# Eight heads' key sums inverted together on 128x128, and GpSimd dividing in the output's stage

## The chip, the cores and the metric

The kernel runs on one core of a Trainium2 chip. The metric is the device time of one execution in microseconds; of a kernel the median of several runs is given. The profile is that of one execution, taken by the hardware profiler. The engines are called PE (TensorE, matmuls), DVE (VectorE), ACT (ScalarE), POOL (GpSimd) and SP (SyncE, which in this kernel issues nearly every transfer).

## The reference

Two attention blocks of the same input sizes (S = 2048 rows, D = 1024 columns, 32 heads of 32 columns, fp32) are computed and mixed by a gate:

```python
def _A_ref(x, wqkv, wo):                       # linear attention
    q, k, v = ...                              # x @ wqkv, cut into heads
    phi = lambda t: jnp.where(t > 0, t + 1, jnp.exp(t)) + 1e-6
    pq, pk = phi(q), phi(k)
    kv = einsum("bhsd,bhse->bhde", pk, v);  z = einsum("bhsd->bhd", pk)
    o = einsum("bhqd,bhde->bhqe", pq, kv) / (einsum("bhqd,bhd->bhq", pq, z)[..., None] + 1e-6)
    return o.reshape(B, S, D) @ wo
def _B_ref(x, wqkv, wo):                       # softmax attention
    scores = einsum("bhqd,bhkd->bhqk", q, k) * Dh ** -0.5
    return einsum("bhqk,bhkd->bhqd", softmax(scores), v).reshape(B, S, D) @ wo
g = sigmoid((A_x * gate_w).sum(-1, keepdims=True))
return g * _A_ref(A_x, ...) + (1 - g) * _B_ref(B_x, ...)
```

The change concerns the division of softmax in block B: each head's product of exponentials and v has to be divided, per query row, by the sum of that row's exponentials over the keys (the "key sum").

## The kernel before

**Precision.** A product of fp32 matrices is made of three matmuls on parts: an operand is cast to fp32r (`hi`, L252, on ACT), the rest is taken by a subtraction (`lo`, L253, on DVE), and hi x hi, hi x lo and lo x hi are added up in one PSUM bank (`three`, L146 to L148). So every operand that arrives as plain fp32 needs a cast on ACT and a subtraction on DVE before PE can use it.

**Stages.** First come the projections of V, Q and K (L407 to L409, L446 to L448, up to about 500 us). Then a long stage, up to about 2690 us, in which four streams are laid between one another by a planner in the program: `linear()` (block A's projections, kv products and outputs, 144 units of matmuls, its output part `ra` per block of 128 rows stored at L823), `maxima()` (scores whose row maxima DVE takes, L887 and L892), `heads_()` (scores again, L1038, exponentials on ACT, L1042, and the products with v, L1136 in `attend`) and, at the end, `output()`. The planner keeps an estimated clock for each engine (`T`), a ring of PSUM banks with the time at which each is free (`take`, `give`), and a list of deferred DVE work with earliest times and ranks (`later`, `defer`, `fill`). It writes out the order of the instructions for all engines when the program is built; on the chip each engine then works its own list in that order.

**Mixing A's weights.** Between units, `mix()` multiplies the heads' kv matrices with A's output weights (L649), four banks at a time. It is called when four banks are free and a part of the weights has been loaded (`mix_ready`). Its results are stored to `wa` (L657) and the next part of the weights is loaded over the last one (L632). Both go through SP.

**SP.** All these transfers stand in SP's one list. A transfer whose source isn't ready holds up all that follow it.

**A head's end before the change.** `finish(h)` sums the exponentials over the keys by matmuls with ones (L940), 128x512 in one bank: partition j*32 + e holds query chunk j, the same sum for all 32 values of e. `invert` (L947) turns it into reciprocals in four DVE instructions of 128x128, and `store` (L950) multiplies the head's output `avs` (copied from PSUM by ACT at L1144) by them and sends it to DRAM (`oB`, four transfers, L952). For the last head, 31, the four pieces are multiplied one by one (L957) and go to the output stage from SBUF. These DVE instructions are deferred work of rank 3.

**The output stage.** For each of 16 blocks of 128 rows, `load_o` loads oB's first 896 columns (L1171; `KF`, heads 0 to 27) and `ra` (L1172), `load_all` the last 128 columns (L1184 for heads 28 to 30, L1189 for head 31; `KL`). `split_o` makes the hi and lo operands in `xo_t`, `gate` takes the sigmoid from x (loads L1205, DVE L1213 to L1219, ACT L1216) and scales ra with it (L1221), `out_pe` does 48 matmuls into two banks, `out_done` adds the parts on DVE (L1242) and stores (L1243). For blocks 0 and 1 the first 896 columns are multiplied while the last head is being finished, then come `gate(0)`, `gate(1)`, the split of the last 128 columns of both, and their matmuls; for the other blocks, the operand of block n+1 is split at the top of iteration n.

Of the kernel before, what the change touches and what calls it, by code (L numbers as in the profile page):

```python
# [18 lines left out]
P = 128  # L19
DH = 32  # L20
# [25 lines left out]
def kernel(  # L46
# [35 lines left out]
    def f32r(ap):  # L82
# [16 lines left out]
            for p in range(2)]  # L99
    ra_d = [dram.tile([P, D], F32, name=f"ra{t}") for t in range(NT)]  # L100

    ident = sb.tile([P, P], F32, name="ident")
# [11 lines left out]
    mneg = [sb.tile([P, NT], F32, name=f"mneg{i}") for i in range(2)]  # L114
    mh = sb.tile([NT, P], F32R, name="mh")
    ml = sb.tile([NT, P], F32R, name="ml")
# [590 lines left out]
    def linear():  # L707
        extra = iter(())
        coming_w = deque()
        for n, (i, t) in enumerate(units):  # L710
# [19 lines left out]
            for k in range(NK):  # L730
# [88 lines left out]
            else:  # L819
# [3 lines left out]
                nc.sync.dma_start(ra_d[t][:, c * C:(c + 1) * C], res)  # L823
        over["lin"] = True
        load_all()

# [100 lines left out]
    o_near = [False]  # L927
    f_left = []
    finished = [-1]

    def finish(h, accs):

        g, r = divmod(h, 4)
        finished[0] = h
        b = take()
        pl = bank[b]
        end = use("pe", AV * len(accs) + (AV_SWITCH if h == H - 1 else 0.0), free[b])
        for n, acc in enumerate(accs):
            for j in range(NJ):
                nc.tensor.matmul(pl[j * DH:(j + 1) * DH, :], ones[:, :DH], acc[:, j * C:(j + 1) * C],  # L940
                                 start=(n == 0), stop=(n == len(accs) - 1))

        rows = slice(r * DH, (r + 1) * DH)

        def invert(i):
            sl = slice(i * P, (i + 1) * P)
            nc.vector.reciprocal(pl[:, sl], pl[:, sl])  # L947

        def store(_):
            nc.vector.tensor_mul(avs, avs, pl)  # L950
            for j in range(NJ):
                nc.sync.dma_start(oB_d[j * TPC:(j + 1) * TPC, rows, g, :].rearrange("t p c -> p t c"),  # L952
                                  avs[j * DH:(j + 1) * DH, :].rearrange("p (t c) -> p t c", c=P))

        def store_part(i):
            sl = slice(i * P, (i + 1) * P)
            nc.vector.tensor_mul(avs[:, sl], avs[:, sl], pl[:, sl])  # L957
            o_there[0] = (i + 1) * NJ
            load_all()

        fns = [(lambda _, i=i: invert(i), 0.87) for i in range(TPC)]
        if h < H - 1:
            fns.append((store, 0.6))
        else:
            fns = [f for i in range(TPC) for f in (fns[i], (lambda _, i=i: store_part(i), 0.33))]
        f_left[:] = chain(fns, end, 3)
        give(b, 0.0, f_left)
# [35 lines left out]
    def heads_():  # L1003
# [57 lines left out]
        for items in pr_left:  # L1061
            need(items)
        xo_t[1] = big_tile(PR[slot(H - 1, NT - 6)], F32R)
        over["head"] = True
        load_all()

    pr_end = [0.0] * NPR

    def attend(h, lacc):
# [34 lines left out]
        def sums(t):  # L1104
# [5 lines left out]
            else:  # L1110
                if t:
                    end = l_end[0] = first(pr_end[idx(1)]) if t == 1 else more(t, pr_end[idx(t)])
                    for u in ((0, 1) if t == 1 else (t,)):
                        pr_free[idx(u)] = max(pr_free[idx(u)], end)
                items = [defer(lambda _: own(t), pr_end[idx(t)], 0.08 + (S - qp) / 960, 2, adds[-1] if adds else None)]
            adds.extend(items)
# [3 lines left out]
        def av(t0, t1):  # L1120
# [18 lines left out]
            if t == NT - 1:  # L1139
                assert finished[0] == h - 1  # L1140
                need(f_left)
                o_near[0] = last
                free[4] = use("act", 0.49, end)
                nc.scalar.copy(avs, av_b)  # L1144
                accs = [lacc, pr(t)] if last else [lacc]
                (tasks if last else ends).append((lambda: both(bank_at(), ended(adds), l_end[0]),
                                                  lambda: finish(h, accs)))
# [11 lines left out]
    xo_ready = [0.0] * NT  # L1159
    xo_t = [xp_t[len(units) % 2], None, xp_t[(len(units) + 1) % 2], None]  # L1160
    split_done = set()
# [12 lines left out]
    def load_all():  # L1174
# [10 lines left out]
        while o_rest[0] < min(o_main[0], o_there[0]):  # L1185
# [3 lines left out]
            nc.sync.dma_start(o_part(n, KL)[LAST, 0], avs[j * DH:(j + 1) * DH, i * P:(i + 1) * P])  # L1189

    def split_o(n, ks):
# [3 lines left out]
        xo_ready[n] = use("dve", 0.06 + 1.05 * size, use("act", 0.2 + 0.8 * size, T["pe"]))  # L1195
        split(blocks(dst, 0)[:, ks], blocks(dst, 1)[:, ks], o_part(n, ks), nc.vector)
# [51 lines left out]
    def output():  # L1248
# [28 lines left out]
        RING.extend((4, 7))  # L1277
        xo_t[3] = big_tile(LACC[(H - 1) % 2], F32R)
# [130 lines left out]
```

## Time and profile before

| what | value |
|---|---|
| runs | 2872.09, 2873.7, 2874.22 us; median 2873.7 |
| profiled execution | 2873.77 us, of which the span is 2872.0 us |
| mean granted clock of PE | 0.996 |
| PE busy | 2846.1 us, 99% of the span |
| DVE busy | 2239.1 us, 78% |
| POOL busy | 1854.1 us, 65% |
| ACT busy | 1617.8 us, 56% |

A row of a group gives line, engine, operation, output and input, shape and count, then busy time in us and the mean of one in ns, then the engine's idle time just before them and what ended it. A row of waits reads "who waits <- for whom: us in total, times, longest". A row of a timeline gives start, length, engine, line and operation; a count x4 joins neighbours. A row of windows gives the stretch, its length, each engine's busy time in the order PE, PEld, DVE, ACT, POOL with the count of instructions, then PE's granted clock, the DMA engines' share and GB/s.

### The profile page before, as it was taken

What the parts mean: (1) busy time and instruction counts of PE and PEld (TensorE: products, weight loads), DVE (VectorE), ACT (ScalarE), POOL (GpSimd) and SP (SyncE); (2) the same over time, 40 slices, a digit from 0 to 9 for tenths busy, and PEclk for the clock granted to TensorE, in tenths of its full rate; (3) what the DMA queues carried; (4) which work ended last, traced back from release to release, by engine and by line L of the source; (5) the groups of instructions that cost most, each with busy time, mean ns of one, the idle gap of its engine ahead of it and who ended that gap; (6) DMA issues with size and microseconds to landing.
All of it is one profiled execution on the core that took longest, in us unless ns stands there. A gap on an engine that the chain in (4) does not pass through costs nothing.

```text
span 2872.0 us, 44436 instructions
## 1 busy us (share of the span) xinstructions
PE 2846.1 (99%) x15744; PEld 2036.8 (71%) x15744; DVE 2239.1 (78%) x3775; ACT 1617.8 (56%) x3007; POOL 1854.1 (65%) x646
## 2 busy tenths in 40 slices
PE   9999999999999999999999999899999999999999
PEld 8888888666666666666666666566766666666687
DVE  7667656788888888888888888778888888886643
ACT  5334321666666667666666666566666656656421
POOL 1212220778898889888988887578778877885000
PEclk9999999999999999999999999999999999999999
DMA  5956764332333233333332235554465344524663
GB/s 179 284 174 212 247 201 152 121 93 92 108 89 92 89 101 110 90 92 92 120 93 90 76 120 168 173 185 145 135 195 167 114 137 133 144 88 143 213 219 105
DMA packets 302498, 400.57 MB, mean 139 GB/s; under 512 B 92682, under 2 KB 185354, under 8 KB 299146
## 3 DMA queue, kind: packets, MB, share of 16 engines
q1 hardware_dynamic: 302276, 397.73, 44.8%
q8 instruction: 124, 2.03, 0.3%
q14 instruction: 98, 0.80, 0.1%
HBM read 287.57 MB, written 108.79 MB: 138 GB/s over the span
## 4 chain that ended last, share of the span: by engine, by line
PE 96%; DMA 2%; DVE 1%; ACT 0%; issue 0%; SPq 0%; ACTq 0%; DVEq 0%
PE bank L1038 16%; PE bank L887 16%; PE bank L1136 15%; PE bank L146 11%; PE bank L148 11%; PE bank L147 11%; PE bank L407 4%; PE bank L409 4%; PE bank L408 4%; PE bank L446 1%; PE bank L940 1%; PE bank L447 1%; PE bank L448 1%; DMA big<-xs 1%; PE bank L693 0%; PE bank L584 0%
## 5 line engine op out<-in xcount | busy, mean ns | idle before, releaser
L1089 POOL TENSOR_TENSOR big<-big,big 128x1536 f32<-128x1536 f32 (+1 forms) x434 | 1556.4, 3586 | 188.9 <-ACT big L1042 166.7
L892 DVE TENSOR_REDUCE mx<-bank 128x1 f32<-128x512 f32 x2048 | 1311.4, 681 | 319.6 <-PE bank L887 315.1
L1042 ACT ACTIVATE big<-bank 128x512 f32<-128x512 f32 x2048 | 1180.6, 601 | 524.8 <-PE bank L1038 455.6
L1038 PE MATMUL bank<-big,big 128*128 128x512 f32 x2048 | 810.7, 397 | 2.7 <-ACT big L1042 2.6
L887 PE MATMUL bank<-big,big 128*128 128x512 f32 x2048 | 803.6, 392 | 3.2 <-ACT mid L342 2.9
L146 PE MATMUL bank<-big,big 128*128 128x512 f32 x1408 | 552.7, 393 | 5.7 <-DMA big<-xs 3.4
L148 PE MATMUL bank<-big,big 128*128 128x512 f32 x1408 | 550.9, 391 | 1.0 <-DMA big<-oA 0.6
L147 PE MATMUL bank<-big,big 128*128 128x512 f32 x1408 | 550.6, 391 | 0.0
L1038 PEld LDWEIGHTS bank<-big,big 128*128 128x128 f32 x2048 | 384.6, 188 | 159.7 <-issue 62.0
L1136 PE MATMUL bank<-big,mid 128*32 128x512 f32 x4096 | 461.1, 595 | 0.0
L887 PEld LDWEIGHTS bank<-big,big 128*128 128x128 f32 x2048 | 385.4, 188 | 87.4 <-ACT big L1042 3.7
L1136 PEld LDWEIGHTS bank<-big,mid 128*32 128x32 f32 x4096 | 127.9, 110 | 266.2 <-issue 266.2
L146 PEld LDWEIGHTS bank<-big,big 128*128 128x128 f32 x1408 | 264.6, 188 | 71.0 <-ACT big L1042 4.3
L148 PEld LDWEIGHTS bank<-big,big 128*128 128x128 f32 x1408 | 264.8, 188 | 57.6 <-DMA big<-oA 1.0
L147 PEld LDWEIGHTS bank<-big,big 128*128 128x128 f32 x1408 | 264.5, 188 | 55.3
L1098 DVE TENSOR_TENSOR bank<-bank,big 128x512 f32<-128x512 f32 (+1 forms) x434 | 280.6, 647 | 7.8 <-ACT big L1042 6.1
L1085 POOL TENSOR_TENSOR big<-big,big 128x1536 f32<-128x1536 f32 (+1 forms) x31 | 111.6, 3601 | 253.0 <-ACT big L1042 135.5
L253 DVE TENSOR_TENSOR big<-mid,big 128x512 fp32r<-128x512 f32 x216 | 153.0, 732 | 80.5 <-ACT big L252 80.5
L386 POOL TENSOR_TENSOR mid<-mid,mid 128x512 f32<-128x512 f32 x16 | 20.6, 1291 | 276.7 <-DVE big L253 250.6
L252 ACT CAST big<-mid 128x512 fp32r<-128x512 f32 x216 | 130.2, 624 | 95.8 <-POOL mid L387 54.0
L407 PE MATMUL bank<-big,big 128*128 128x512 f32 x448 | 174.3, 389 | 0.0
L408 PE MATMUL bank<-big,big 128*128 128x512 f32 x448 | 174.3, 389 | 0.0
(103 smaller groups left out, 1981.9 us busy)
## 6 DMA issues: line engine op xcount, KB each, us to landing
big<-xs SPq DMA_DIRECT2D x208, 512.0 KB
qk<-mid SPq DMA_DIRECT2D x128, 256.0 KB
big<-oA SPq DMA_DIRECT2D x64, 512.0 KB
big<-qk SPq DMA_DIRECT2D x96, 256.0 KB
big<-qk SPq DMA_DIRECT2D x384, 64.0 KB
mid<-in_b_wqkv SPq DMA_DIRECT2D x88, 256.0 KB
xs<-big SPq DMA_DIRECT2D x64, 256.0 KB
oA<-mid SPq DMA_DIRECT2D x64, 256.0 KB
```

The source lines that it names most:

```text
L146: yield nc.tensor.matmul(ps, sh, mh_, start=(kt == 0), stop=False)
L147: yield nc.tensor.matmul(ps, sh, ml_, start=False, stop=False)
L148: yield nc.tensor.matmul(ps, sl, mh_, start=False, stop=(kt == NK - 1))
L407: nc.tensor.matmul(ps, sh, mh_, start=(i == 0), stop=False)
L408: nc.tensor.matmul(ps, sh, ml_, start=False, stop=False)
L887: nc.tensor.matmul(bank[b], q[:, t * P:(t + 1) * P], k[:, j * C:(j + 1) * C], start=True, stop=True)
L892: nc.vector.tensor_reduce(m[:, t, j:j + 1], bank[b], AX.X, ALU.max)
L1038: nc.tensor.matmul(bank[b], k[:, t * P:(t + 1) * P], q[:, j * C:(j + 1) * C], start=True, stop=True)
L1042: nc.scalar.activation(pr_t[i][:, j * C:(j + 1) * C], bank[b], AF.Exp, scale=SCALE)
L1089: nc.gpsimd.tensor_add(lacc[:, :qp], lacc[:, :qp], pr(t)[:, :qp])
L1098: nc.vector.tensor_add(lacc[:, qp:] if t == NT - 1 else l_b[:, :n], l_b[:, :n], src)
L1136: nc.tensor.matmul(av_b[j * DH:(j + 1) * DH, :], v[:, t, :], pr(t)[:, j * C:(j + 1) * C], start=(t == 0), stop=(t == NT - 1))
```

## The change

For heads 0 to 30 the four reciprocals and the multiplication by them leave the head's end. `avs` goes to oB undivided, right behind ACT's copy. The bank with the key sums is copied to SBUF by ACT (`l_sb`), and one row of 2048 sums goes to DRAM (`l_d`, four pieces of 512). After heads 7, 15, 23, 27 and 30 the rows of the group (8, 8, 8, 4 and 3 heads) are loaded back flat, on all 128 partitions (128 columns for eight heads), inverted by one DVE instruction, and stored to `r_d`.

In the output's stage, `load_r` loads the reciprocals of a block, each row spread over the 32 partitions of its head (four transfers of 32x7x128 for KF, three of 32x128 for KL), into the half of `xo_t` that will later hold lo; `scale_o` multiplies the block's oB part by them on GpSimd (128x896 and 96x128), and the cast and subtraction follow as before. Head 31 is still divided by pieces on DVE. `xo_t[1]` and `xo_t[3]` move to the two tiles of `w_t`, `mh` and `ml` share a tile, the split of block 0 stands at the last step of the last linear unit in place of the second, and block 1's is no longer in that unit.

```diff
 def finish(h, accs):
-        def store(_):
-            nc.vector.tensor_mul(avs, avs, pl)
-            for j in range(NJ):
-                nc.sync.dma_start(oB_d[j * TPC:(j + 1) * TPC, rows, g, :].rearrange("t p c -> p t c"),
-                                  avs[j * DH:(j + 1) * DH, :].rearrange("p (t c) -> p t c", c=P))
+        if h < H - 1:
+            end = use("act", 0.5, end)
+            give(b, end)
+            nc.scalar.copy(l_sb, pl)
+            nc.sync.dma_start(l_d[h].rearrange("(j c) -> j c", c=C),
+                              l_sb.rearrange("(j e) c -> j e c", e=DH)[:, 0, :])
+            first, count = next(((a, n) for a, n in zip(R_FIRST, R_COUNT) if a + n == h + 1), (0, 0))
+            if count:
+                part = l_sb[:, :count * S // P]
+                flat = [...]                        # the group's rows of l_d and of r_d, flat over 128 partitions
+                nc.sync.dma_start(part, flat[0])
+                def back(_):
+                    nc.vector.reciprocal(part, part)
+                    nc.sync.dma_start(flat[1], part)
+                    r_there[0] = first + count
+                    load_rest()
+                r_left[:] = [defer(back, end + 6.0, 0.15 + count * 0.11, 2)]
+            return
         fns = [(lambda _, i=i: invert(i), 0.87) for i in range(TPC)]
-        if h < H - 1:
-            fns.append((store, 0.6))
...
 def attend(h, lacc):
                 nc.scalar.copy(avs, av_b)
+                if not last:
+                    g, r = divmod(h, 4)
+                    for j in range(NJ):
+                        nc.sync.dma_start(oB_d[...], avs[...])      # the four stores that `store` had
...
+    def load_r(n, ks):
+        need(r_left)
+        t = t_order[n]
+        part = blocks(xo_t[n % len(xo_t)], 1)[:, ks]
+        for r in range(4 if ks == KF else 3):
+            src = r_d.rearrange("(k r) s -> r k s", r=4)[r, ks, t * P:(t + 1) * P]
+            nc.sync.dma_start(f32(part[r * DH:(r + 1) * DH]),
+                              src.unsqueeze(0).to_broadcast([DH, ks.stop - ks.start, P]))
+    def load_rest():
+        if over["lin"] and r_there[0] == H - 1 and not r_rest[0]:
+            r_rest[0] = True
+            load_r(0, KL)
+            load_r(1, KL)
+            for n in (2, 3):
+                load_r(n, KF)
+                load_r(n, KL)
+    def scale_o(n, ks):
+        rows = slice(0, P if ks == KF else LAST.start)
+        part = o_part(n, ks)[rows]
+        r = f32(blocks(xo_t[n % len(xo_t)], 1)[rows, ks])
+        nc.gpsimd.tensor_mul(part, part, r)
+        return use("pool", 0.1 + (ks.stop - ks.start) * 0.3)
     def split_o(n, ks):
+        if ks == slice(0, NK):
+            end = max(scale_o(n, KF), scale_o(n, KL))
+        else:
+            end = scale_o(n, ks)
...
 # in linear(), the last unit
                 if k == 1 and n + 1 == len(units):
+                    load_r(0, KF)
+                if k == NK - 1 and n + 1 == len(units):
                     split_o(0, slice(0, NK - 1))
-                if k == NK // 2 and n + 1 == len(units) and over["head"]:
-                    split_o(1, slice(0, NK - 1))
...
 # behind linear()'s last unit
         over["lin"] = True
+        load_r(1, KF)
+        load_rest()
         load_all()
...
 # output(), the loop over blocks
                 split_o(n + 1, slice(0, NK))
+                if n + 2 < NT:
+                    load_r(n + 2, KF)
+                    load_r(n + 2, KL)
```

**How it moves the instructions.** On PE the count of instructions stays, and 148 rows of them stand elsewhere. The place that matters is the first mix on the weights' second half (L649 before, L652 after), in the middle of the long stage; `big_3758` and `big_3760` are the weights, `big_3752` and the like the exponentials of a head. Before:

```order
L940 MATMUL bank_244<-big_3756,ones 32x512 x4
L1136 MATMUL bank_247<-big_3752,mid_242 32x512 x4
L1136 MATMUL bank_247<-big_3753,mid_242 32x512 x4
L1136 MATMUL bank_247<-big_3754,mid_242 32x512 x4
L1136 MATMUL bank_247<-big_3755,mid_242 32x512 x4
L1136 MATMUL bank_247<-big_3749,mid_242 32x512 x4
L693 MATMUL bank_248<-ident,mid_234 128x128 x4
```

and after:

```order
L946 MATMUL bank_246<-big_3758,ones 32x512 x4
L1154 MATMUL bank_249<-big_3754,mid_244 32x512 x4
L1154 MATMUL bank_249<-big_3755,mid_244 32x512 x4
L1154 MATMUL bank_249<-big_3756,mid_244 32x512 x4
L652 MATMUL bank_251<-big_3760,kvb 32x512 x4
L652 MATMUL bank_247<-big_3760,kvb 32x512 x4
L652 MATMUL bank_246<-big_3760,kvb 32x512 x4
L652 MATMUL bank_245<-big_3760,kvb 32x512 x4
L1154 MATMUL bank_249<-big_3757,mid_244 32x512 x4
L1154 MATMUL bank_249<-big_3751,mid_244 32x512 x4
```

The mix now stands within the group of attention products in which no mix stood before; before, it came with the next such group.

On SP, the load of the weights' next part, with the stores that stand ahead of it (`xs` are operands of the linear stream, `oA` its outputs). Before:

```order
L657 DMA wa_0_0_166<-mid_239 4x32x512
L657 DMA wa_0_0_162<-big_3758 4x32x512
L559 DMA big_213<-xs_9_72 128x1024
L559 DMA big_213<-xs_9_88 128x1024
L700 DMA oA_6_101<-mid_237 128x512
L700 DMA oA_6_117<-mid_238 128x512
L657 DMA wa_0_0_166<-mid_229 4x32x512
L657 DMA wa_0_0_162<-big_3758 4x32x512
L657 DMA wa_0_0_166<-mid_230 4x32x512
L632 DMA big_3758<-in_a_wo 128x512 x4
```

and after:

```order
L660 DMA wa_0_0_166<-mid_232 4x32x512
L562 DMA big_214<-xs_8_71 128x1024
L562 DMA big_214<-xs_8_87 128x1024
L917 DMA big_224<-m_both 1x16x128 x2
L562 DMA big_215<-xs_9_72 128x1024
L562 DMA big_215<-xs_9_88 128x1024
L703 DMA oA_6_101<-mid_239 128x512
L703 DMA oA_6_117<-mid_240 128x512
L635 DMA big_3760<-in_a_wo 128x512 x4
```

Four of the five stores of `wa` that stood just ahead of the load are no longer there.

On SP, the start of the output's stage, from the stores of the last two `ra` blocks on. Before:

```order
L823 DMA ra_184<-mid_236 128x512
L823 DMA ra_185<-mid_239 128x512
L1171 DMA big_3749<-oB 128x896
L1172 DMA big_3749<-ra_178 128x1024
L1171 DMA big_3750<-oB 128x896
L1172 DMA big_3750<-ra_182 128x1024
L1184 DMA big_3749<-oB 96x128
L1184 DMA big_3750<-oB 96x128
L1202 DMA zrep<-in_gate_w 128x1024
L1205 DMA mid_237<-in_x 128x512
```

and after, up to the loads of oB:

```order
L826 DMA ra_184<-mid_238 128x512
L1222 DMA big_214<-r 32x7x128 x4
L1213 DMA big_3760<-mid_242 32x128
L1213 DMA big_3755<-mid_242 32x128
L826 DMA ra_185<-mid_241 128x512
L1222 DMA big_226<-r 32x7x128 x4
L1222 DMA big_214<-r 32x128 x3
L1222 DMA big_226<-r 32x128 x3
L1222 DMA big_215<-r 32x7x128 x4
L1222 DMA big_215<-r 32x128 x3
L1222 DMA big_227<-r 32x7x128 x4
L1222 DMA big_227<-r 32x128 x3
```

Behind these rows come the loads of oB and ra for three blocks (two before), of the last 128 columns, and then `zrep` and `in_x`. So 24 transfers of r, and those of one more block, stand between the last store of ra and the gate's inputs.

More of the change, by code (lines that the diff above doesn't have):

```diff
@@ L100 @@
     ra_d = [dram.tile([P, D], F32, name=f"ra{t}") for t in range(NT)]
+    l_d = dram.tile([H, S], F32, name="l")
+    r_d = dram.tile([H, S], F32, name="r")
     ident = sb.tile([P, P], F32, name="ident")
@@ L114 @@
     mneg = [sb.tile([P, NT], F32, name=f"mneg{i}") for i in range(2)]
-    mh = sb.tile([NT, P], F32R, name="mh")
-    ml = sb.tile([NT, P], F32R, name="ml")
+    m_both = sb.tile([DH + NT, P], F32R, name="m_both")
+    mh, ml = m_both[:NT], m_both[DH:]
+    l_sb = sb.tile([P, C], F32, name="l_sb")
     dn = [sb.tile([P, C // DH], F32, name=f"dn{i}") for i in range(2)]
@@ L928 @@
     f_left = []
+    r_left, r_there = [], [0]
+    R_FIRST, R_COUNT = (0, 8, 16, 24, 28), (8, 8, 8, 4, 3)
     finished = [-1]
     def finish(h, accs):
-        g, r = divmod(h, 4)
         finished[0] = h
@@ L941, in finish @@
                                  start=(n == 0), stop=(n == len(accs) - 1))
-        rows = slice(r * DH, (r + 1) * DH)
         def invert(i):
@@ L959, in store_part @@
             load_all()
+        if h < H - 1:
[7 more added lines that the diff above has]
+                part = l_sb[:, :count * S // P]
+                flat = [m[first:first + count].rearrange("h s -> (h s)").rearrange("(p e) -> p e", p=P)
+                        for m in (l_d, r_d)]
+                nc.sync.dma_start(part, flat[0])
[6 more added lines that the diff above has]
+            return
         fns = [(lambda _, i=i: invert(i), 0.87) for i in range(TPC)]
-        if h < H - 1:
-            fns.append((store, 0.6))
-        else:
-            fns = [f for i in range(TPC) for f in (fns[i], (lambda _, i=i: store_part(i), 0.33))]
+        fns = [f for i in range(TPC) for f in (fns[i], (lambda _, i=i: store_part(i), 0.33))]
         f_left[:] = chain(fns, end, 3)
@@ L1062, in heads_ @@
             need(items)
-        xo_t[1] = big_tile(PR[slot(H - 1, NT - 6)], F32R)
         over["head"] = True
@@ L1067 @@
     pr_end = [0.0] * NPR
+    own_last = [None]
     def attend(h, lacc):
@@ L1114, in sums @@
                         pr_free[idx(u)] = max(pr_free[idx(u)], end)
-                items = [defer(lambda _: own(t), pr_end[idx(t)], 0.08 + (S - qp) / 960, 2, adds[-1] if adds else None)]
+                items = [defer(lambda _: own(t), pr_end[idx(t)], 0.08 + (S - qp) / 960, 2, own_last[0])]
+                own_last[0] = items[0]
             adds.extend(items)
@@ L1144, in av @@
                 nc.scalar.copy(avs, av_b)
+                if not last:
+                    g, r = divmod(h, 4)
+                    for j in range(NJ):
+                        nc.sync.dma_start(
+                            oB_d[j * TPC:(j + 1) * TPC, r * DH:(r + 1) * DH, g, :].rearrange("t p c -> p t c"),
+                            avs[j * DH:(j + 1) * DH, :].rearrange("p (t c) -> p t c", c=P))
                 accs = [lacc, pr(t)] if last else [lacc]
@@ L1159 @@
     xo_ready = [0.0] * NT
-    xo_t = [xp_t[len(units) % 2], None, xp_t[(len(units) + 1) % 2], None]
+    xo_t = [xp_t[len(units) % 2], w_t[0], xp_t[(len(units) + 1) % 2], w_t[1]]
     split_done = set()
@@ L1194, in split_o @@
         size = (ks.stop - ks.start) * P / 1000.0
-        xo_ready[n] = use("dve", 0.06 + 1.05 * size, use("act", 0.2 + 0.8 * size, T["pe"]))
+        xo_ready[n] = use("dve", 0.06 + 1.05 * size, use("act", 0.2 + 0.8 * size, T["pe"], end))
         split(blocks(dst, 0)[:, ks], blocks(dst, 1)[:, ks], o_part(n, ks), nc.vector)
@@ L1277, in output @@
         RING.extend((4, 7))
-        xo_t[3] = big_tile(LACC[(H - 1) % 2], F32R)
+        load_rest()
         split_o(0, KL)
```

1 line of the change is left out of this document (added).

## The prediction

> **What bounds the kernel now.** I read the page's engine shares first, then the chain of waits, TensorE's own waits, and last the two stretches that the change touches most. The profiled execution took 2873.77 us, its span is 2872.0 us, so 1.8 us lie around the span; the runs' median is 2873.7, and a sum made against the profiled time is a sum against the median.
>
> ```profile
> PE 2846.1 (99%) x15744; PEld 2036.8 (71%) x15744; DVE 2239.1 (78%) x3775; ACT 1617.8 (56%) x3007; POOL 1854.1 (65%) x646
> PE 96%; DMA 2%; DVE 1%; ACT 0%; issue 0%; SPq 0%; ACTq 0%; DVEq 0%
> ```
>
> TensorE is busy for 2846.1 of 2872.0 us, and 96% of the chain that ends last is TensorE. Nothing that makes another engine's work shorter can win more than the 25.9 us in which TensorE stands still, plus what a slow clock costs after such a stop. So the question is only where TensorE waits, and where it will wait. Of TensorE's waits these are the largest:
>
> ```profile
> PE bank L649 <- DMA big<-in_a_wo: 7.5, 1, 7.5
> PE bank L146 <- DMA big<-xs: 3.4, 2, 2.0
> PE bank L887 <- ACT mid L342: 2.9, 1, 2.9
> PE bank L1038 <- ACT big L1042: 2.6, 1, 2.6
> ```
>
> One wait of 7.5 us, for the second part of A's output weights, is a third of all idle time. Nobody waits for DVE by name here, though DVE is 78% busy. (A measurement of this kernel tells a change from none at about 0.2%, 5.7 us.)
>
> **Part 1: what is taken from DVE.** Per head, heads 0 to 30, four reciprocals and one multiplication go, and one copy on ACT comes.
>
> ```profile
> L947 DVE RECIPROCAL bank<-bank 128x128 f32<-128x128 f32 x128 | 123.3, 963 | 3.5 <-PE bank L940 0.4
> L950 DVE TENSOR_TENSOR mid<-mid,bank 128x512 f32<-128x512 f32 x31 | 21.3, 686 | 1.0
> L1144 ACT COPY mid<-bank 128x512 f32<-128x512 f32 x32 | 18.8, 588 | 151.7 <-PE bank L1136 136.0 <-DMA big<-qk 15.7
> ```
>
> DVE loses 31 x (4 x 0.963 + 0.686) = 140.7 us; ACT gains 31 x 0.59 = 18 us, and it is 56% busy. Five group reciprocals on 128x128 or less give DVE back under 5 us. On the path this is worth only what TensorE waited for these instructions. Its waits name none of them; its weight loads do:
>
> ```profile
> PEld bank L1038 <- DVE bank L947: 5.9, 7, 0.8
> PEld bank L1038 <- DVE mid L950: 2.1, 6, 0.5
> ```
>
> Weight loads overlap matmuls, and these pauses of at most 0.8 us are seen as no wait of the matmuls. I take 0; the bounds are 0 and -8.0 (all of both rows). The 11.4 us of shorter waits are covered by TensorE's queue of other streams' matmuls; were that cover gone, the same 8 us would be what is lost. The added ACT copy holds up exponentials by 0.6 us once per head, behind the same cover.
>
> **Part 2: the second load of A's weights.** Here the planner's order moves. The bank with the key sums is free after one ACT copy, not after four reciprocals in DVE's queue, so the first mix on the new half has its four banks one group of attention products earlier, and among the nine or ten places on SP just ahead of the load stands one wa store, where five stood. Before:
>
> ```profile
> 1814.04 0.51 SPq L657 DMA_DIRECT2D wa<-mid  x1
> 1814.61 0.64 SPq L657 DMA_DIRECT2D wa<-big  x1
> 1815.29 1.82 SPq L657 DMA_DIRECT2D wa<-mid  x1
> 1817.15 8.91 SPq L632 DMA_DIRECT2D big<-in_a_wo  x4
> 1818.32 3.64 PE L1136 MATMUL bank<-big,mid 128*32 128x512 f32 x32
> 1829.48 3.79 PE L649 MATMUL bank<-big,kvb 32*32 32x512 f32 x32 [7.53 <-DMA big<-in_a_wo]
> ```
>
> SP reaches the load at 1817.15, just ahead of the matmuls that need it, and needs 8.9 us to get its four parts away, because the wa stores and the other writes ahead of it have not landed. In the changed order the mix that empties the buffer runs a group earlier, and the load has the products of other streams between it and its users. Behind the stall the clock falls:
>
> ```profile
> 1820.00:1830.00 10.00, 2.48 (x22) 0.58 (x15) 1.05 (x3) 0.31 (x1) 1.97 (x1) 0.78 0.58 191
> 1830.00:1834.00 4.00, 4.00 (x36) 0.81 (x38) 0.00 (x0) 0.61 (x2) 0.00 (x0) 0.50 0.06 18
> 1834.00:1838.00 4.00, 4.00 (x26) 1.88 (x19) 2.87 (x5) 2.99 (x6) 0.00 (x0) 0.78 0.17 35
> 1838.00:1842.00 4.00, 4.00 (x19) 3.31 (x18) 3.44 (x7) 2.48 (x5) 0.00 (x0) 1.00 0.83 270
> ```
>
> The seventh number from the left, behind the POOL column, is the granted clock: 0.50 for 4 us and 0.78 for 4 more, which is 4 x 0.50 + 4 x 0.22 = 2.9 us of lost full-speed time. So this stall costs 7.5 + 2.9 = 10.4 us. I take it as wholly gone, -10.4; the bounds are 0 (the wait comes back in another place) and -13.8 (the 3.4 us for xs go too). The Trainium skill, "TensorE: Matmul & The Clock Gate", section on the HAM clock gate, says that the clock halves after about 3.4 us without work and comes back after about 3.4 us of it; by that such a stall would cost 1.7 us on top, where the windows above show 2.9; the gain here and the loss in part 3 would both be 1.2 us smaller, and the sum the same.
>
> **Part 3: the start of the output stage.** This is where the change adds. Before, SP goes from the last two stores of ra almost straight to the gate's inputs:
>
> ```profile
> 2686.63 7.83 SPq L823 DMA_DIRECT2D ra<-mid  x2
> 2697.85 0.38 SPq L1172 DMA_DIRECT2D big<-ra  x1
> 2698.28 0.91 SPq L1184 DMA_DIRECT2D big<-oB  x2
> 2699.78 2.71 SPq L1205 DMA_DIRECT2D mid<-in_x  x4
> 2706.99 0.69 DVE L1213 SCALAR_TENSOR_TENSOR mid<-mid,zrep 128x512 f32<-128x512 f32 x1 [6.91 <-DMA mid<-in_x]
> 2712.43 1.43 ACT L252 CAST big<-big 128x128 fp32r<-128x128 f32 x3
> 2712.76 0.50 PE L146 MATMUL bank<-big,big 128*128 128x512 f32 x1
> 2691.85 1.77 ACT L252 CAST big<-big 128x896 fp32r<-128x896 f32 x2
> 2692.84 0.50 PE L146 MATMUL bank<-big,big 128*128 128x512 f32 x1 [1.90 <-ACT big L252]
> ```
>
> DVE works both gates before it splits the last 128 columns of blocks 0 and 1, and ACT does the gates' parts before its casts. From in_x's landing (2706.99) to the first product of those columns (2712.76) it is 5.8 us, and TensorE comes to that product just then, with no slack: the 84 products of the two blocks, from 2692.84, cover it exactly.
>
> In the changed order 24 transfers of r stand on SP between ra15's store and the loads of oB and ra, then a third pair of these loads (block 2), and only then zrep and in_x. What is queued behind them on SP is everything that the output's start needs. The terms:
>
> (a) SP gets past ra15's store later, because its copy on ACT now stands behind block 0's cast, which waits for GpSimd's multiplication, which waits for the first four transfers of r. GpSimd's 128x896 isn't in the trace; from two sizes of the same operation,
>
> ```profile
> L783 POOL TENSOR_TENSOR mid<-mid,mid 128x256 f32<-128x256 f32 x60 | 44.1, 736 | 20.5 <-DVE mid L778 20.3
> L386 POOL TENSOR_TENSOR mid<-mid,mid 128x512 f32<-128x512 f32 x16 | 20.6, 1291 | 276.7 <-DVE big L253 250.6 <-DMA qk<-mid 26.1
> ```
>
> it is 2.17 ns an element, 736 + 640 x 2.17 = 2.1 us. SP's four issues end near 2689, they land 4.5 us later (in_x: 2706.99 less 2702.49), so 2693.5 + 2.1 + 0.9 (half of the two casts' 1.77) + 0.6 for ra's copy = 2697.1 where it was 2694.5: +2.6, bounds 0 and +5.
>
> (b) 24 issues at 0.455 us (the pair in 0.91): +10.9. Bounds from the rows above: 0.38 gives +9.1, in_x's 0.68 gives +16.3. A transfer of 32x7x128 moves little, so SP's issuing and not the bytes sets this.
>
> (c) The third pair of loads is 128x896 and 128x1024, 0.98 MB. The stretch that follows moves data at the rate that this row shows last:
>
> ```profile
> 2700.00:2720.00 20.00, 20.00 (x89) 16.28 (x88) 10.07 (x32) 5.75 (x10) 0.00 (x0) 1.00 0.83 286
> ```
>
> 0.98 MB at 286 GB/s is 3.4 us, which waits in front of in_x; issued alone it would be 0.8. I take +2.8.
>
> In_x lands 2.6 + 10.9 + 2.8 = 16.3 us later, at 2723.3, and the last columns' products start at 2729.1. TensorE itself starts block 0 with its cast, 3.7 us later (2696.5), and would be there at 2716.4: it waits some 12.7 us, its own late start is swallowed in that, and the clock falls as in part 2, +2.9. Part 3 is +19.2, with bounds of +10 (0 + 9.1 + 0.8, no loss of clock) and +27 (5 + 16.3 + 3.4 + 2.9 = 27.6, rounded down, since the first two can't both be at their worst on one queue).
>
> **Part 4: the steady output loop.** From block 3 on, each block has seven transfers of r, 3.2 us of SP, and on GpSimd 2.1 + 0.5 us. From out(n-1)'s end it is 3.2 + 4.5 + 2.6 + about 1.0 + 1.2 for cast and subtraction = 12.5 us to block n+2's operand, plus what SP waits for out's store. TensorE has two blocks to work meanwhile: 89 products in 20 us is 0.225 us each, 96 of them 21.6 us. It is hidden, with 9 us of cover; if the cover is gone, each microsecond over counts some twelve times. I take 0.
>
> **The sum.** 2873.8 + 0 - 10.4 + 19.2 + 0 = 2882.6; as a time, 2882.
>
> **The rivals.**
>
> *The gain at the second weight load does not come* (the load is again late, or its stores now stand in front of xs loads). For it: SP carries 143 more transfers, and 31 rows of key sums are written where the stores of oB were. Against it: the four parts are issued a group earlier. 2873.8 + 19.2 = 2893.
>
> *Not slower: the relief is worth more than the tail.* SP had waited long for the multiplication that is gone, in front of all other loads:
>
> ```profile
> SPq L952 <- DVE mid L950: 233.6, 29, 14.7
> ```
>
> If that queue was the hidden cause of the waits for xs (3.4), and of the weight loads' pauses (8.0), these go as well, and with r issued at 0.38 us (-1.8): 2882.6 - 13.2 = 2869.4, and down to 2866 when SP also isn't held up at ra15. It decides from the point at which 9 us of stalls go beyond the one of part 2; against it stands that all stalls together are 25.9 us, of which part 2 has 7.5 already.
>
> *The output loop can't keep up.* GpSimd reads SBUF in every block beside DVE's subtraction and gates. The view of line 253 shows what that does:
>
> ```profile
> L253 DVE TENSOR_TENSOR big<-mid,big x216: 679/685/1545, 4.5 to 2692.0; 128x512 fp32r<-128x512 f32 x108
> L253 DVE TENSOR_TENSOR mid<-big,mid x48: 691/692/693, 69.0 to 400.9; 128x512 fp32r<-128x512 f32 x48
> ```
>
> The same subtraction takes up to 1545 ns in the stretches where GpSimd works, and 693 at most where it doesn't: up to 0.9 us, and for a longer GpSimd operation up to its length. Two such meetings per block (2 x 2.1) and stores that come back late (2 us) eat 6 of the 9 us; if 1.5 us a block is then missing in 12 blocks, it is +18: 2900. The Trainium skill, "SBUF — State Buffer", section "Who interferes with whom", says that a DVE instruction with two SBUF inputs and a GpSimd instruction that reads SBUF shut each other out for a whole instruction; the two rows above agree with it.
>
> **How the numbers follow.** The forecast has 0.60 (its own range is 2876 to 2889), the lost gain 0.12, not slower 0.16, the loop 0.12. Faster by over 0.2% (under 2868) is most of the not-slower case, 0.12. Within 0.2% (2868 to 2879.4) is the forecast's lower end, 0.12, the rest of the not-slower case, 0.04, and a loop that falls short with a small tail, 0.02: 0.18. Slower is 0.70. The range is 2867 to 2894: it leaves out half of the not-slower case and most of the loop's.
>
> **What would show it.** In the profile after: TensorE's wait for in_a_wo near 1820 is gone and the granted clock stays at 1.00 there; on SP a run of 24 loads of r stands ahead of zrep and in_x, some 11 us long; DVE's idle time before the first gate is over 20 us, put down to in_x; TensorE waits 8 to 16 us for the cast of the last 128 columns, and shows 0.50 behind it; TensorE's busy time is as before but for the clock, and DVE's is near 2239.1 - 140.7 + 5 = 2103. The prediction is wrong if in_x lands less than 8 us later, if the a_wo wait is still there, or if TensorE waits in the blocks from 3 on.

## The result, and the profile after

The changed kernel takes 2968.3 us (2965.4 to 2971.6, four executions) where the kernel before takes 2873.1: the ratio is 1.0332, with a 95% interval of 1.0314 to 1.035. It is 95 us slower. The forecast was 2882, the range ended at 2894. The sign was right, the size was not. One execution in the first experiment took 11981.2 us at a granted clock of 0.227 and isn't counted; all other times are of undisturbed executions.

The page's engine shares and the chain of waits of the changed kernel:

```profile
PE 2871.6 (97%) x15744; PEld 2045.9 (69%) x15744; DVE 2111.5 (71%) x3625; ACT 1638.7 (55%) x3038; POOL 1895.0 (64%) x678
DMA 6%; SPq 1%; DVE 1%; issue 0%; PE 0%; ACT 0%; POOL 0%; POOLq 0%; ACTq 0%; DVEq 0%
DMA big<-r 4%; DMA out<-big 2%; SPq L1222 0%; DMA mid<-in_x 0%; DVE mid L1269 0%; DVE big L256 0%; DMA big<-oB 0%; ACT big L255 0%; SPq L1213 0%; SPq L1208 0%; PE bank L151 0%; SPq L1196 0%; DVE big L1298 0%; PE bank L150 0%; PE bank L149 0%
```

TensorE stood for 96% of the chain before. Now the chain that ends last is TensorE at 0%, and transfers of r lead it. (The view follows the end back through the output's stage, so its shares don't reach the long stage.) DVE's busy time fell as planned, from 2239.1 to 2111.5 us, and that is no gain. TensorE's waits:

```profile
PE bank L149 <- ACT big L255: 63.9, 12, 15.6
PE bank L149 <- DMA big<-xs: 7.1, 2, 6.8
PE bank L151 <- DVE big L256: 4.2, 8, 0.5
PE bank L149 <- DMA big<-oB: 3.9, 1, 3.9
```

The wait for `in_a_wo` (7.5 us) is gone. One for `xs` of nearly the same length has come, and 63.9 us of waits for the casts of the output's operands.

The time can be split at three places of TensorE's timeline: the last product of the last linear unit (at 2690.55 before, 2687.41 after), the first product of blocks 0 and 1's last columns (2712.76 and 2744.58), and the last product of all (2867.75 and 2961.68).

| stretch | before, us | after, us | difference |
|---|---|---|---|
| start to the last linear product | 2690.55 | 2687.41 | -3.1 |
| from there to the last columns' products | 22.2 | 57.2 | +35.0 |
| from there to the last product | 155.0 | 217.1 | +62.1 |
| behind it | 4.2 | 4.3 | +0.1 |

The spans are 2872.0 and 2966.0 us: +94.0. So a third of the loss is the output's start, and two thirds are the output's loop. The -3.1 is no gain that can be told: in the six experiments below that change little or nothing ahead of that point, it lies between 2687.0 and 2693.6 us. SP at the start, with the first rows of DVE and TensorE that waited for it, after:

```profile
2699.16 0.34 SPq L826 DMA_DIRECT2D ra<-mid  x1
2699.61 20.74 SPq L1222 DMA_DIRECT2D big<-r  x24
2726.96 0.32 SPq L1196 DMA_DIRECT2D big<-ra  x1
2732.97 0.36 SPq L1258 DMA_DIRECT2D zrep<-in_gate_w  x1
2734.42 2.78 SPq L1261 DMA_DIRECT2D mid<-in_x  x4
2738.47 0.78 DVE L1269 SCALAR_TENSOR_TENSOR mid<-mid,zrep 128x512 f32<-128x512 f32 x1 [23.87 <-DMA mid<-in_x]
2744.58 0.79 PE L149 MATMUL bank<-big,big 128*128 128x512 f32 x1 [15.60 <-ACT big L255]
```

The 24 loads of r take SP 20.7 us, 0.86 each, and the loads behind them take another 14 until in_x's turn. Two turns of the loop, in the chain of waits:

```profile
2761.99 0.44 SPq L1222
2762.48 8.15 DMA big<-r
2770.69 5.40 DMA out<-big
2776.14 0.33 SPq L1196
2776.56 0.38 SPq L1208
2777.00 0.51 SPq L1213
2777.56 0.57 SPq L1222
2778.18 0.44 SPq L1222
2778.67 9.30 DMA big<-r
2788.03 3.92 DMA out<-big
2792.00 0.33 SPq L1196
```

A block takes 15.9 us here (2776.14 to 2792.00) and 16.5 on the average of nine turns, where TensorE needs 10.9. Some nine of them pass from the issue of a load of r to its landing; the stores of `out` come behind that on SP, and the next block's `ra` goes over the tile that `out` is stored from. TensorE isn't in this ring at all. Why SP gets stuck can be read from the issues and landings in the trace: of 1891 transfers none starts before the one eight places ahead of it on SP's list has landed. So a load that lands late soon holds up what comes eight places behind it, here a store of `out`, which starts at 2770.69, after a load of r has landed at 2770.63.

### The profile page after: what moved, and what is told of

The parts are those of the page before. It is cut to its first block, busy times and chain, and to the rows that moved or that the text cites. A ratio compares the mean times of both kernels' runs of the same rounds, so it can differ in the third digit from the quotient of the medians.

```text
span 2966.0 us, 44727 instructions
## 1 busy us (share of the span) xinstructions
PE 2871.6 (97%) x15744; PEld 2045.9 (69%) x15744; DVE 2111.5 (71%) x3625; ACT 1638.7 (55%) x3038; POOL 1895.0 (64%) x678
## 5 line engine op out<-in xcount | busy, mean ns | idle before, releaser
L1054 PE MATMUL bank<-big,big 128*128 128x512 f32 x2048 | 811.0, 398 | 1.2 <-ACT big L1058 1.2
L892 PE MATMUL bank<-big,big 128*128 128x512 f32 x2048 | 804.2, 393 | 6.3 <-ACT mid L345 3.0
L149 PE MATMUL bank<-big,big 128*128 128x512 f32 x1408 | 562.8, 400 | 76.1 <-ACT big L255 63.9
L151 PE MATMUL bank<-big,big 128*128 128x512 f32 x1408 | 560.1, 398 | 4.8 <-DVE big L256 4.2
L150 PE MATMUL bank<-big,big 128*128 128x512 f32 x1408 | 558.5, 397 | 0.1
L151 PEld LDWEIGHTS bank<-big,big 128*128 128x128 f32 x1408 | 269.1, 191 | 69.8 <-DVE big L256 11.4
L1240 POOL TENSOR_TENSOR big<-big,big 128x896 f32<-128x896 f32 (+1 forms) x32 | 40.4, 1283 | 282.8 <-DMA big<-r 83.4
L389 POOL TENSOR_TENSOR mid<-mid,mid 128x512 f32<-128x512 f32 x16 | 20.7, 1292 | 276.6 <-DVE big L256 276.6
L410 PE MATMUL bank<-big,big 128*128 128x512 f32 x448 | 174.3, 389 | 0.0
```

Of the source, the lines that this page charges most:

```text
L149: yield nc.tensor.matmul(ps, sh, mh_, start=(kt == 0), stop=False)
L150: yield nc.tensor.matmul(ps, sh, ml_, start=False, stop=False)
L151: yield nc.tensor.matmul(ps, sl, mh_, start=False, stop=(kt == NK - 1))
L410: nc.tensor.matmul(ps, sh, mh_, start=(i == 0), stop=False)
L892: nc.tensor.matmul(bank[b], q[:, t * P:(t + 1) * P], k[:, j * C:(j + 1) * C], start=True, stop=True)
L1054: nc.tensor.matmul(bank[b], k[:, t * P:(t + 1) * P], q[:, j * C:(j + 1) * C], start=True, stop=True)
```

## The experiments

Two theories stood first. T: the transfers of r are slow, and SP's order turns that into time. P: GpSimd's multiplication, and its exclusion with DVE, lengthen each block (the prediction's third rival).

**Without the multiplication.**

```diff
 def scale_o(n, ks):
-        nc.gpsimd.tensor_mul(part, part, r)
```

> The changed kernel without GpSimd's multiplications in the output's stage (the outputs of heads 0 to 30 stay undivided); r is still loaded. Theory T (the transfers of r: each takes some 2 us of the queue, and everything behind them on SP waits) expects 2955 to 2968 us, with the same 16 us per output block, since GpSimd is not in the chain of the loop. Theory P (GpSimd's multiplication and its exclusion with DVE lengthen each block) expects 12 blocks by 2.5 us and more: 2938 or less.

The one execution that counts took 2964.5 us, hardly below the changed kernel's 2965.4 to 2971.6. TensorE still stops ten times in the loop, by 3.4 to 5.9 us. From the last linear product to the last of all it is 264.8 us, where the changed kernel has 274.3, so the multiplication is at most some 9 of the 97 us that this stretch lost, and most of them lie at its start. P falls.

**Without the loads of r.**

```diff
 def load_r(n, ks):
-            nc.sync.dma_start(f32(part[r * DH:(r + 1) * DH]), src.unsqueeze(0).to_broadcast(...))
```

> The changed kernel without the loads of r in the output's stage (GpSimd multiplies by what lies in the tile); all else stays. T expects the loop back at 10.9 us a block and the whole at 2865 to 2880: 2873 less 10.4 for the weights' wait, plus 6.9 for the new wait for xs, plus some us for GpSimd at the start. P expects 2930 or more.

2882.4 us, ratio 1.0044 (1.0024 to 1.0063); the loop runs without a stop, with the multiplications in it. So some 83 to 86 us lie in the loads of r (83 when each kernel is taken against the kernel before as it ran beside it). It stands 2.4 us above T's range, which had "some us" for the output's start: TensorE still waits 6.1 us for casts there, 4.0 of them ahead of the last columns:

```profile
PE bank L149 <- DMA big<-xs: 6.2, 1, 6.2
PE bank L149 <- ACT big L255: 6.1, 2, 4.0
```

**Why is a transfer of r slow?** It moves 32x7x128, 112 KB, in pieces of 512 bytes; each piece goes to 32 partitions. First the pieces were made larger: r is stored by blocks (row r, block t, then the seven k), so that a partition reads 3584 bytes at once.

```diff
+    rw_d = dram.tile([4, NT, NK - 1, P], F32, name="rw")
...
+                src = rw_d[r, t].rearrange("k s -> (k s)")     # KF; heads 28 to 30 stay in r_d
```

> The changed kernel with r stored in DRAM by blocks, so that a partition's 7x128 values are one piece of 3584 bytes and no longer seven of 512: as many bytes, as many transfers, a seventh of the pieces. If the pieces set the 2 us of a transfer (T by pieces), it falls under 1 us and the kernel to 2880 to 2905. If the bytes or the reading of the same row for 32 partitions set it, it stays at 2955 to 2970.

2891.7 us, ratio 1.0074 (1.0045 to 1.0103): 74 to 77 us back, and no stop in the loop. By this expectation the size of the pieces was the cause.

Beside it, pieces as small as before, but with a row of its own for each partition, from another array (GpSimd then multiplies by other numbers):

```diff
-            src = r_d.rearrange("(k r) s -> r k s", r=4)[r, ks, t * P:(t + 1) * P]
+            rows = qk_d[0][0][t % NK][r * DH:(r + 1) * DH]
+            if ks == KF:
+                src = rows[:, :2044].rearrange("s (k c) -> s k c", c=292)[:, :, :P]
...
```

> The changed kernel with loads of the same shape and piece size (32x7x128, pieces of 512 bytes) that read a row of their own for each partition, from another array (so GpSimd multiplies by other numbers). If reading one row 32 times is what costs, it falls to 2880 to 2905; if the pieces cost, it stays at 2955 to 2970.

2897.5 us. Small pieces are quick too, then. That contradicts the reading of the run before it: by "pieces of 512 bytes are slow" this one should have stayed at 2960. Both have in common that the seven pieces of a partition do not lie 32768 bytes apart, as rows k of `r_d` do (four heads of 2048 floats). So theory S was formed, the stride, against H, 32 readers of the same small piece. Padding alone tells them apart:

```diff
+    rp_d = dram.tile([H - 4, S + P], F32, name="rp")        # rows of 8704 bytes instead of 8192
...                                                          # the reciprocals are stored to it row by row
-            src = r_d.rearrange("(k r) s -> r k s", r=4)[r, ks, ...]
+            src = (rp_d if ks == KF else r_d).rearrange("(k r) s -> r k s", r=4)[r, ks, ...]
```

> The changed kernel with r's rows of heads 0 to 27 in a padded array, so that the seven pieces of 512 bytes that a partition reads lie 34816 bytes apart instead of 32768; each piece is still read by 32 partitions. Theory S (the stride of 32768 bytes puts all pieces of a transfer in one part of the memory) expects the loop back at 10.9 us a block: 2885 to 2900. Theory H (32 readers of the same 512 bytes are what is slow) expects no change: 2955 to 2970.

2895.7 us, ratio 1.0081 (1.0061 to 1.0101): the loads differ from the changed kernel's in nothing but 512 bytes at the end of each row. Two turns of the loop's loads of r on SP in the changed kernel:

```profile
2761.41 3.41 SPq L1222 DMA_DIRECT2D big<-r  x7
2777.56 3.45 SPq L1222 DMA_DIRECT2D big<-r  x7
```

and a turn with the padding:

```profile
2780.12 2.00 SPq L1228 DMA_DIRECT2D big<-rp  x4
2782.22 1.31 SPq L1228 DMA_DIRECT2D big<-r  x3
2783.63 0.84 SPq L1267 DMA_DIRECT2D mid<-in_x  x2
2784.57 0.84 SPq L1305 DMA_DIRECT2D out<-big  x2
2785.51 0.43 SPq L1201 DMA_DIRECT2D big<-oB  x1
2790.47 2.00 SPq L1228 DMA_DIRECT2D big<-rp  x4
2762.00:2784.00 22.00, 22.00 (x98) 18.21 (x98) 8.79 (x22) 4.82 (x6) 5.06 (x4) 1.00 0.78 237
```

The seven loads go out in 3.4 us in both. It is their landing that differs: from the first issue of a block's four loads of 32x7x128 to the last landing it is 12.0 us in the changed kernel and 4.9 with the padding (medians of 12 blocks, from the landings in the traces). With the padding the next turn starts 10.4 us later (the turn before took 11.5); the last row, of the windows view, shows TensorE busy for 22.00 of 22 us. The other half of the test, small pieces with 32 readers lying 528 bytes apart:

```diff
+    rw_d = dram.tile([4, NT, NK - 1, P + 4], F32, name="rw")
+                src = rw_d[r, t, :, :P]
```

> As the kernel with r by blocks, but with 16 bytes of padding behind each 512, so that a partition again reads seven pieces of 512 bytes, which now lie 528 bytes apart; each is read by 32 partitions. S expects it to be as fast as the kernel with pieces of 3584 bytes: 2885 to 2900. H, in the form that small pieces with many readers are slow wherever they lie, expects 2955 to 2970.

2897.0 us. S holds as far as the stride goes: neither small pieces nor 32 readers are slow by themselves, and the loads are slow only where the pieces lie 32768 bytes from each other. Whether many readers are needed beside the stride wasn't tried: the one run with a row for each reader had another stride as well. Why this stride is slow no run here shows.

**The order at the output's start.** With the slow loads out of the way, the kernel with pieces of 3584 bytes still loses 21 us. Its loads were put in another order:

```diff
         load_r(1, KF)
+        for n in range(NF):
+            load_g(n)                         # zrep and in_x, ahead of the other loads of r
         load_rest()                           # now r of the last columns and of block 2, load_all(), r of block 3
...
-                if k == 1 and n + 1 == len(units):
+                if k == 0 and n + 1 == len(units):
                     load_r(0, KF)
```

> The kernel with r in pieces of 3584 bytes (2891.7 us), with the loads at the output's start in another order on SP: the gate's inputs right behind block 1's r, then r of blocks 0 and 1's last columns and of block 2, then oB and ra, then r of block 3; block 0's r one step earlier. If the queue ahead of in_x is what TensorE waited for before the last columns (11.2 us and the clock behind it), 2877 to 2881. If it waits for something else of the start (GpSimd, the head's last pieces), 2887 or more.

2890.1 us: nearly nothing, against 2877 to 2881. The wait ahead of the last columns is gone; it was 10.8 us in the kernel that this run starts from:

```profile
PE bank L150 <- DMA mid<-in_x: 10.8, 1, 10.8
```

But these stops are there with the new order:

```profile
2697.68 0.79 PE L150 MATMUL bank<-big,big 128*128 128x512 f32 x1 [6.00 <-ACT big L256]
2725.71 0.50 PE L150 MATMUL bank<-big,big 128*128 128x512 f32 x1 [2.86 <-ACT big L256]
2751.73 0.54 PE L150 MATMUL bank<-big,big 128*128 128x512 f32 x1 [3.15 <-ACT big L256]
```

The first is the wait ahead of block 0, which stays at 6.0 (before the change 1.9). The other two stand ahead of blocks 2 and 4, where there was no stop. So the start is 11.3 us shorter (28.7 in place of 40.0) and the rest 6.9 longer (164.2 in place of 157.4). From the last linear product to the last of all it is 192.9 us in place of 197.4; the profiled execution was as much longer in the middle. So this expectation was a miss: most of what is won at one place of the queue is lost at a later one.

**The middle.** The a_wo wait is gone, the xs wait has come. The wait's place on TensorE after the change, and the windows around it:

```profile
1846.01 0.77 PE L149 MATMUL bank<-big,big 128*128 128x512 f32 x1 [6.75 <-DMA big<-xs]
1835.00:1842.00 7.00, 4.26 (x19) 3.19 (x17) 5.33 (x11) 5.16 (x10) 6.84 (x3) 1.00 0.98 197
1842.00:1848.00 6.00, 1.99 (x7) 1.74 (x8) 0.00 (x0) 0.33 (x1) 2.85 (x1) 0.52 0.72 256
```

The DMA engines are 0.98 busy ahead of the stop. Among the transfers ahead of xs are the stores of `wa`, 256 KB each. In the trace of the kernel before, three of them land at 1823.16, 1825.72 and 1828.40 us, some 2.6 apart, where two `oA` stores of the same size land at 1819.95 and 1820.58. Theory W: their backlog is what both stalls are made of.

```diff
             def store(p, src, r=r):
-                nc.sync.dma_start(wa_d[p][a][c][:, r * DH:(r + 1) * DH, :], f32(src))
+                for i in range(HK):
+                    nc.sync.dma_start(wa_d[p][a][c][i, r * DH:(r + 1) * DH, :], f32(src)[i * DH:(i + 1) * DH])
```

On the kernel with pieces of 3584 bytes:

> The kernel with r in pieces of 3584 bytes, with each store of wa (4x32x512, some 2.5 us of the DMA engines where 128x512 takes 0.6) cut in four stores of 32x512. Theory W (the wait for xs near 1840, which took the place of the one for a_wo, is the backlog of these stores) expects that wait (6.6 us, and the clock behind it) to go: 2880 to 2884. If the undivided oB stores or the mere count of transfers cause it, 2890 or more.

2882.1 us, ratio 1.0039 (1.0027 to 1.0052): 9.6 us below the 2891.7. The xs waits of TensorE are not gone, as W had expected, but 4.8 us in three pieces, 2.6 the longest, where they were 7.2 with one of 6.6:

```profile
PE bank L150 <- DMA big<-xs: 4.8, 3, 2.6
```

The same edit on the kernel before, alone:

> The kernel before with the stores of wa cut in four, and nothing else. W expects the a_wo wait (7.5 us and 2.9 of clock) and the smaller waits behind it (7 us) to go: 2855 to 2862. If the stores' size in time is not the cause, 2869 or more, since SP issues 48 more... 96 transfers more at 0.45 us.

2861.0 us, ratio 0.9961 (0.9947 to 0.9976). TensorE's largest wait there is now

```profile
PE bank L649 <- DMA big<-in_a_wo: 3.2, 1, 3.2
```

and the two later stops for xs, 3.4 us together, are gone. This kernel is faster than both the one before and the changed one. So W holds in the main: in both kernels the shorter stores win some 10 us. They don't remove the stalls: 3.2 us for a_wo are left here and 4.8 for xs there.

**One part of the change alone.** The bank is given free by ACT's copy, as in the change; the division stays on DVE.

```diff
+        if h < H - 1:
+            end = use("act", 0.5, end)
+            give(b, end)
+            nc.scalar.copy(l_sb, pl)
+            pl = l_sb                          # the reciprocals and the multiplication read the copy
...
```

> The kernel before with one part of the change alone: ACT copies the key sums of heads 0 to 30 to SBUF and gives the bank free; the four reciprocals and the multiplication stay on DVE and read the copy. The first mix then stands where the changed kernel has it. If the stall has only moved from a_wo to xs with that (W), the middle wins 1 to 3 us: 2867 to 2871, and the xs wait is seen near 1840. If the undivided stores of the changed kernel caused the xs wait, the full 10 us are won: 2859 to 2863.

2872.9 us, ratio 1.0002 (0.9992 to 1.0011): no change that can be told, above the 2867 to 2871 that W named and far above the 2859 to 2863 of the other reading. The first mix stands where the changed kernel has it, the a_wo wait of 7.5 us near 1829 is gone, and TensorE's waits are now led by these:

```profile
PE bank L1046 <- DVE mx L893: 4.5, 3, 2.7
PE bank L147 <- DMA big<-xs: 3.3, 2, 3.1
```

The waits for DVE's row maxima are new. Those for xs are in sum what they were before (3.4 us); the one of 3.1 us stands ahead of the product that waited 2.0 us before the change and 6.8 in the changed kernel. So the bank's early release by itself wins nothing, and the wait that it removes comes back only in part at xs. How much of the 6.8 us in the changed kernel is due to its undivided stores of oB stays open.

**The edits together.** Both edits to the kernel before:

> The kernel before with two edits: key sums copied by ACT so that their bank is free early (division stays on DVE), and the stores of wa cut in four. If with shorter stores the earlier mix is worth what is left of the a_wo wait (3.2 us and some clock), 2855 to 2859, below the 2861 of the cut stores alone. If new waits for DVE (4.5 us in the kernel with the first edit alone) eat that, 2860 to 2864.

2863.4 us, ratio 0.997 (0.996 to 0.998). The waits for DVE (4.6 us) remain, and the early bank adds nothing to the shorter stores: this interval and that of the cut stores alone overlap. And all three mends on the changed kernel:

> The changed kernel with all three mends: r in pieces of 3584 bytes, the new order of loads at the output's start, wa's stores cut in four. If the mends add up, 2891.7 less 9.5 less 4 (what the order won between the last linear unit and the end): 2876 to 2880. Slower than before in any case, by what the start of the output still loses to loads of r and GpSimd.

2878.8 us, ratio 1.0025 (1.0014 to 1.0035), within what was expected. Of the 95 us some 88 are mended. From the last linear product to the last of all it is still 194.9 us, where it was 177.2, and the shorter stores pay for a part of that. The largest stop left there:

```profile
2687.54 0.80 PE L150 MATMUL bank<-big,big 128*128 128x512 f32 x1 [6.23 <-ACT big L256]
```

Block 0 waits for r, GpSimd and the cast one after the other, where it waited for the cast alone. Most of that is r: without its loads, but with GpSimd's multiplication, the same stop was 2.1 us.

## Why the prediction was right and wrong

**Part 4, put at 0, measured +62.1: the step that failed, and the largest miss.** Its chain of 12.5 us took 4.5 us for r's landing, from in_x's row, and the sentence "It is hidden, with 9 us of cover" rests on that. In the chain of waits the landing measures 7.0 to 10.6, and a block's four loads of 32x7x128 take 12.0 us from the first issue to the last landing. With the rows padded that is 4.9, so the term was right for loads of the usual speed, and what it missed is the stride. The chain had also been taken as one that starts with out(n-1) and has two blocks of time. In the trace SP's list closes it to a ring of one block: r, then the store of `out` behind it, then `ra` over the tile stored, then the next r. A ring has no cover of two blocks. (With the usual landing the ring is no limit: TensorE is busy for 22.00 of 22 us.) The third rival had the place and 2900, but by the wrong mechanism: without the multiplication, 2964.5. Of the prediction's own signs of being wrong the last came: TensorE waits in the blocks from 4 to 13.

**Part 3, +19.2 us, of which 16.3 lie ahead of the last columns' products; measured there +35.0.** In_x lands 31.5 us later (2738.47 after, 2706.99 before), and the stretch begins 3.1 us earlier. (a) was put at +2.6: SP passed ra15's store at 2699.5 in place of 2694.5, +5.0, the upper bound. (b) was put at 24 x 0.455 = 10.9 and measured 20.7, beyond its upper bound of 16.3. The sentence that failed is "A transfer of 32x7x128 moves little, so SP's issuing and not the bytes sets this". It was right about the bytes, but a third thing set it, the landing: with eight transfers under way SP waits, and single issues then start two microseconds apart in the trace (2704.96, 2706.93 and 2708.93). (c) was put at +2.8 and measured 8.8 for the same reason: in_x went out 14.1 us behind the last r, where it had been 5.3 behind ra15's store. GpSimd's piece, 2.1 us by two other sizes of the same operation, measured 2.08.

**Part 2, -10.4 us: the wait named did go, the gain did not come.** The middle ended 3.1 us earlier, which is within what executions of the same middle differ by. The step that failed is "I take it as wholly gone". TensorE, arriving earlier, met a backlog of stores some 16.5 us further on, at xs, in a wait of 6.8 us with a granted clock of 0.52 around it. Its lower bound of 0, "the wait comes back in another place", is nearly what happened, and the first rival had its cause half right, with 0.12. That slow stores of `wa` make up most of both stalls is shown by the runs with cut stores (-9.6 and -10 us). What else the early mix meets is open, as the run with the early bank alone shows.

**Part 1, what is taken from DVE: put at 0, and nothing here speaks against it.** DVE is busy for 127.6 us less (135.7 had been worked out). The nearest pair has an early bank and cut stores on both sides: with the division on DVE TensorE reaches the last linear product at 2682.5 us, without it at 2681.2 and 2680.9. That difference is within the scatter too.

**How far the working holds once r's stride is mended.** In the padded kernel SP's terms measure (a) 4.0, (b) 12.2 and (c) 4.0, each 1.2 to 1.4 us more than predicted, and in_x lands 17.4 us later, against 16.3. Its start costs 39.9 us from the last linear product to the last columns, where the kernel before took 22.2: +17.6. Its loop takes 157.6 us against 155.0, which is near the 2.9 us of slow clock that part 3 had. With part 2 at nothing, the sum of the prediction is 2873.8 + 19.2 = 2893, its first rival; the padded kernel takes 2895.7, and is 24 us above the kernel before as it ran beside it. So the terms of SP's issues and the start were well sized for transfers of the usual speed. The price of a transfer that the trace did not hold was taken from the nearest row, without a bound for a slower landing.

**Sign and chances.** Slower had 0.70 and came, but not by the balance that was forecast: part 2's gain did not come, and over 70 of the 95 us are a cost that no case and no bound had. The padded kernel is slower as well, so the sign doesn't hang on the stride alone.

**Readings of the prediction that don't hold.** SP carries 153 more transfers, not 143. No row shown gives the "11.4 us of shorter waits", and the sum doesn't use them. The two rows of line 253 don't part stretches with and without GpSimd, which is busy for 85 us between 69 and 401. One by one in the trace, the subtractions of the first row that meet no GpSimd instruction take 695 ns at most, and of the 24 that meet one the longest takes 1545, so the conclusion stands.

## What to carry to other kernels

A load that the trace has not yet shown has two prices, its issue and its landing, and where a queue waits for the transfer eight places ahead, as here, a slow landing turns into slow issues. Bound both, and look at the addresses: where a load's pieces lie 32768 bytes apart, as here, try padding before anything else. When a stall is named after a late load, ask what the DMA engines were doing in the time before: moving the consumer earlier won nothing here, while making the transfers ahead of it shorter won 10 us.

## What was not expected of the hardware

Pieces of 512 bytes at 32768 bytes from each other, read by 32 partitions: 0.86 us of SP per load in the run of 24, four loads in 12.0 us, and 16.5 us per output block. At 34816 bytes, or 528, or in one piece: four loads in 4.6 to 4.9 us and 10.9 us per block, with equal bytes and equal counts of loads. The difference is some 70 to 77 us of the kernel.

A store of 4x32x512 is slow for its 256 KB, and four of 32x512 are not: from issue to landing it is 10 to 11 us for the one and 1.7 for each of the four (medians of the kernel before and of the one with the shorter stores). It was worth 10 us in each of two kernels, though SP issues 96 transfers more. The Trainium skill, "DMA: Bandwidth & Descriptors", section "Why a DMA increments its semaphore by 16 and not by 1", says that a transfer is spread over the largest number of engines, at most 16, that divides its slowest dimension on both sides: 4 here, and 16 for a store of 32 rows. The traces agree with it: the semaphore of each of the 32 stores of 4x32x512 is updated once 0.4 us after the issue and then four more times, up to the landing, and that of each of the 128 stores of 32x512 sixteen times. For r the rule finds no fault, since its slowest dimension is 32 and each of its 112 loads shows 16 updates, and the padding shows that another cause was at work there.
